# The values of the last two tiles of batch 0: by transfers into block-diagonal chunk slots instead of shift products

## The chip, the cores and the metric

The kernel runs on 1 core of one Trainium2 chip. The metric is device time in microseconds (us), as the median of several runs. A profile is one execution of its own; its time is told beside its span (first to last recorded instruction).

## What is computed

Chunked attention, then a gated feed-forward (B=4 batches, H=8 heads, S=768 rows, D=64; chunks of 32 rows):

```python
for c in range(S // 32):
    c_start = 32 * c
    l_start, r_end = max(0, c_start - 16), min(S, c_start + 32 + 8)
    k_full = concatenate([mem_k, k[:, :, l_start:r_end]], axis=2)   # 8 memory rows
    v_full = concatenate([mem_v, v[:, :, l_start:r_end]], axis=2)
    scores = (q_c @ k_full.T) / sqrt(D)
    out[:, :, c_start:c_start + 32] = softmax(scores) @ v_full
x = out.transpose(0, 2, 1, 3).reshape(3072, 512)
y = (relu(x @ w_gate) * (x @ w_val)) @ w_out                        # 512 -> 1536 -> 512
```

## The kernel before

**Tiles and blocks.** Attention is done in 24 tiles of 128 rows (4 chunks each, 6 tiles per batch, all 8 heads at once). The feed-forward takes blocks of 2, 2, 2, 4, 4, 4, 4 and 2 tiles. Blocks 0 and 1 (tiles 0 to 3) run interleaved by groups of hidden chunks (`GROUPS`, line 52), so that each part of the weights is used by both as it arrives; then come their output products, then block 2 (tiles 4 and 5), block 3 (tiles 6 to 9) and so on.

**A tile's steps.** q and k are transposed on TensorE (lines 239, 280), scores go to PSUM (line 311), VectorE and ScalarE do the softmax (lines 324 to 354), p is transposed (line 360), `values` multiplies it with v (lines 376 to 390), and `x_copy` writes the block's input. `first` (line 409) makes the gate and value products, `relu` and `gate` (lines 415, 421) read them, `second` (line 434) makes the output products with `w_out`.

**v.** A chunk needs 56 rows of context plus 8 memory rows for each of two heads: 128 partitions for a pair of heads. For batches 1 to 3 `v_bd[b % 2]` holds, per head pair and chunk, a block-diagonal 128x128 matrix, filled by transfers (`load_v_rows`), copies on chip (`upper`) and the memory rows (`mem_rows`); `values` then needs one product per pair and chunk, 16 per tile (line 390). Batch 0 goes another way: `load_v_tile` (line 201) brings v in natural order, 128 rows at a time; `shift` (line 217) multiplies it with a shifted band matrix so that each chunk's context starts at partition 0 or 64; `shift_copy` writes the result to `v_q`, which lies inside `v_bd[0]`. `values` then does 4 products with the pattern of the memory rows `vmem_0` (line 376) and 32 products with `v_q` (line 383) per tile. `v_bd[0]` must be zero outside the slots before batch 2 uses it: the `z0` operations (line 136 or 134) do that, those of head pairs 2 and 3 early, those of 0 and 1 after `values` of tile 5.

**The order of the work.** Everything is written in an order that a small planner in the kernel (`schedule`, line 700) works out: each operation has engines with planned durations, a priority, dependencies, and rooms of buffers that it takes and gives. Engines execute their streams in that order; TensorE gets `idle_product`s in planned gaps up to 18 us. Loads are a list of their own, issued in order by GpSimd (POOL in the profile): q and k of batch 0 as pairs of tiles (`load_pair`, tag `qk_p`), v tiles, weights by group (`load_gate_val`), memory values, then the steps of `ORDER` (line 55), in which an integer is so many q or k loads of later tiles, `w0` and `w1` are the two halves of `w_out`, `v1` is v of batch 1. The planner takes a load as landed a fixed time after its turn on the queue; for a load that is neither a gate weight nor `vl`, that time is 2.4 up to the 44th load and 4.0 behind it (line 758). The v and q/k loads share 8 buffers (tag `qk_b`).

Of the kernel before, what the change touches and what calls it, by code (L numbers as in the profile page):

```python
# [11 lines left out]
BF16 = mybir.dt.bfloat16  # L12
# [7 lines left out]
def kernel(  # L20
# [12 lines left out]
    nc = tc.nc  # L33

    B, H, S, D = q.shape
# [5 lines left out]
    CH = 32  # L41
    NCH = S // CH
    HP = H // 2
    TPB = S // 128
# [4 lines left out]
    CTX = 16 + CH + 8  # L49
    NSET = 2  # L50
# [1 line left out]
    GROUPS = [(0, 2), (2, 6), (6, 9), (9, 12)]  # L52
    BAND0 = 48
    UT = 3
    ORDER = [5, 'w0', 'w1', 'v1', 15, 'v2', 'm2', 6, 'v3', 10, 'm3']

    LATE_QK, LATE_P = 11, 10

# [3 lines left out]
    const = ctx.enter_context(tc.tile_pool(name="const", bufs=1))  # L62
# [15 lines left out]
    def copy(eng, o, i):  # L78
        if eng is nc.scalar:
            nc.scalar.copy(o, i)  # L80
        else:
            eng.tensor_copy(o, i)  # L82


    band = const.tile([128, BAND0 + 176], F16, name="band")
    ident_h = band[:, BAND0:BAND0 + 128]
    ident_b = const.tile([128, 128], BF16, name="ident_b")
    idle = const.tile([128, 256], BF16, name="idle")
    ident_f = const.tile([128, 128], F32, name="ident_f")
    w_gate_sb = const.tile([128, NFC, DFF], F16, name="w_gate_sb")  # L90
    w_val_sb = const.tile([128, NFC, DFF], F16, name="w_val_sb")
# [4 lines left out]
    vmem_0 = const.tile([128, HP, 2 * D], F16, name="vmem_0")  # L96
    v_bd = [const.tile([128, HP, NCH, 2 * D], F16, name=f"v_bd_{s}") for s in range(NSET)]
    vmem_f = v_bd[0][:, HP - 1].rearrange("p c d -> p (c d)").bitcast(F32)[:, 0:HP * 2 * D].rearrange(
        "p (h d) -> p h d", h=HP)
    v_q = v_bd[0][:, 0:2].rearrange("p h c d -> p (h c d)").rearrange("p (h c d) -> p h c d", h=HP, d=D)  # L100
    v_n = {}
    warm = const.tile([1, 8], F32, name="warm")

# [34 lines left out]
    def idle_product(N):  # L138
        if "idle" not in TMP:
            TMP["idle"] = fps.tile([128, 512], F32, tag="fps", name="idle_ps")  # L140
        nc.tensor.matmul(TMP["idle"][:, 0:N], lhsT=idle[:, 0:128], rhs=idle[:, 0:N], start=True, stop=True)  # L141
# [55 lines left out]
    def load_v_tile(t):  # L197
        if t % 2 == 0:
            x = ldpool.tile([128, 2, H, D], F16, tag="qk_b", name="v_n")
            v_n[t], v_n[t + 1] = x[:, 0], x[:, 1]  # L200
        nc.gpsimd.dma_start(
            v_n[t],
            bass.AP(tensor=v.tensor, offset=v[0, 0, 128 * t, 0].offset,
                    ap=[[D, 128], [S * D, H], [1, D]]))

    def shift(c0):
        ps = TMP["sh", c0] = fps.tile([128, 2, HP, D], F32, tag="fps", name="vs_ps")
        for i in range(2):
            t, g = divmod(c0 + i, 4)
            parts = [(t, BAND0 + CH * g - 16)]  # L210
            if g == 0 and t:
                parts.append((t - 1, BAND0 + 112))
            if g == 3 and t < TPB - 1:
                parts.append((t + 1, BAND0 - 48))
            for n, (src, x) in enumerate(parts):
                for par in range(2):
                    nc.tensor.matmul(ps[D * par:D * par + D, i], lhsT=band[:, x:x + 64],  # L217
                                     rhs=v_n[src][:, HP * par:HP * par + HP, :],
                                     start=(n == 0), stop=(n == len(parts) - 1))

    def shift_copy(c0, eng):
# [148 lines left out]
    def values(a):  # L370
        b, t = divmod(a, TPB)
        ps = TMP["x", a] = aps.tile([128, HP, 128], F32, tag="aps", name="xT_ps")
        x = PT.pop(a)
        if b == 0:
            for hp in range(HP):
                nc.tensor.matmul(ps[:, hp, :], lhsT=vmem_0[:, hp, :], rhs=x[:, hp, :],  # L376
                                 start=(hp == 0), stop=False, skip_group_check=True)
            for hp in range(HP):
                for g in range(4):
                    r = slice(CH * g, CH * g + CH)  # L380
                    for par in range(2):
                        p = D * par
                        nc.tensor.matmul(ps[p:p + D, hp, r], lhsT=v_q[p:p + CTX, hp, 4 * t + g, :],  # L383
                                         rhs=x[p:p + CTX, hp, r], start=False, stop=(hp, g) == (HP - 1, 3),
                                         skip_group_check=True)
            return
        for hp in range(HP):
            for g in range(4):
                r = slice(CH * g, CH * g + CH)
                nc.tensor.matmul(ps[:, hp, r], lhsT=v_bd[b % NSET][:, hp, 4 * t + g, :],  # L390
                                 rhs=x[:, hp, r], start=True, stop=True)

    def x_copy(a, eng):
# [59 lines left out]
    def op(key, eng, fn, deps=(), prio=(0,), take=(), give=(), after=()):  # L453
        ops[key] = dict(eng=eng, fn=fn, deps=list(deps), prio=prio, take=list(take), give=list(give),
                        after=list(after))

    def load(key, n, work, fn, deps=(), take=(), after=()):
        loads.append(dict(key=key, n=n, work=work, fn=fn, deps=list(deps), take=list(take), after=list(after)))
# [7 lines left out]
    engine = {"ACT": nc.scalar, "DVE": nc.vector}  # L466
# [3 lines left out]
    op("idle", {"DVE": 0.2}, lambda e: nc.vector.memset(idle, 0.0), prio=(-10,))  # L470
    for hp in range(HP):
        op(("z1", hp), {"ACT": 1.5} if hp % 2 else {"DVE": 1.4}, lambda e, hp=hp: zero(engine[e], v_bd[1], hp), ["idle"], prio=(-1, hp), after=["warm2", "vmem_f"] + ["ib"] * (hp == 2))
    for hp in (2, 3, 0, 1):
        for c0 in range(0, NCH, 8):
            op(("z0", hp, c0), {"ACT": 0.6, "DVE": 0.55}, lambda e, hp=hp, c0=c0: zero(engine[e], v_bd[0], hp, c0, c0 + 8),
               ["vm0" if hp > 1 else ("v", TPB - 1)], prio=(3, -hp) if hp > 1 else (0.7, hp),
               after=[("v", 3)] + ([("tc", 12, 1)] if (hp, c0) == (1, NCH - 8) else []))
    op("warm", {"DVE": 0.15}, lambda e: nc.vector.memset(warm, 0.0), prio=(-9,))  # L478
    op("warm2", {"ACT": 1.5}, lambda e: nc.scalar.activation(warm, warm, ACT.Exp), ["warm"], prio=(-9,))
    op("vmem_f", {"DVE": 0.55}, lambda e: nc.vector.memset(vmem_f, 0.0), prio=(-8,), after=["warm"])  # L480
# [45 lines left out]
    for a in range(NT):  # L526
# [38 lines left out]
            op(("pc", a), psum16(HP * 128), lambda e, a=a: p_copy(a, engine[e]), [("p", a)], (1, a, 9), ["pT"], ["aps"])  # L565
        else:
            op(("pc", a), {"SP": ISSUE}, lambda e, a=a: p_transfer(a), [("nrm", a)], (0, a), ["pT"], [("pn", min(LAND_P[a], 7.0))])
        if b == 0:
            for c0 in (4 * t, 4 * t + 2):
                need = {c // 4 for c in (c0, c0 + 1)} | {max(c0 - 1, 0) // 4, min(c0 + 2, NCH - 1) // 4}  # L570
                gone = ([t - 1] if c0 % 4 == 0 and t in (2, 4) else []) + ([t] if c0 == NCH - 2 else [])
                op(("sh", c0), {"PE": 0.4}, lambda e, c0=c0: shift(c0), [("vn", n) for n in sorted(need)] + ["ident"],
                   (1, a, 7.5), ["fps"], ["qk"] * len(gone), [("s", t)])
                op(("shc", c0), {"ACT": psum(2 * HP * D)["ACT"]} if t < 2 else psum(2 * HP * D), lambda e, c0=c0: shift_copy(c0, engine[e]), [("sh", c0)],
                   (1, a, 7.6), (), ["fps"], [("exp", 0)] if t == 0 else [])
        blk = block_of[a]
        j = a - starts[blk]
        op(("v", a), {"PE": 0.45 if b else 1.0}, lambda e, a=a: values(a),
           [("pc", a) if a < LATE_P else (("pc", a), LAND_P[a])]
           + ([("vl", b, n) for n in range(2)] + [("up", b, n, m) for n in range(2 * HP) for m in range(t // UT + 1)]  # L580
              + [("ve", b, n) for n in range(2) if last] if b else [("shc", 4 * t), ("shc", 4 * t + 2), "vm0"])
           + ([("mr", b, n) for n in range(2 * HP)] if b else []), (1, a, 10), ["aps"] + (["xT"] if j == 0 else []), ["pT"],
           [("v", a - 1)] if a else [])
        op(("x", a), psum(HP * 128), lambda e, a=a: x_copy(a, engine[e]), [("v", a)], (1, a, 11), (), ["aps"],
# [3 lines left out]
    for rank, (blk, m) in enumerate(seq):  # L588
        n = BLOCKS[blk]
# [44 lines left out]
    def load_w_op(g):  # L634
        for w in range(2):
            for par in range(2):
                load(("w", g, w, par), 256, 0.35 * (GROUPS[g][1] - GROUPS[g][0]), lambda g=g, w=w, par=par: load_gate_val(g, w, par))

    def load_pair_op(r, i):
        load(("pl", r, i), 1024, 1.45, lambda: load_pair(r, i), take=["qk"])  # L640

    def load_v_nat(t):
        load(("vn", t), 1024, 1.05, lambda: load_v_tile(t), take=["qk"] * (1 - t % 2))

    late = [(a, i) for a in range(TPB, NT) for i in (1, 0)]
    load_pair_op(0, 1)
# [10 lines left out]
    load_v_nat(4)  # L657
    load_w_op(1)
    load_w_op(2)
    load_w_op(3)  # L660
    load_pair_op(2, 0)
    load_v_nat(5)
    for par in range(2):
        load(("vm", par), 256, 0.3, lambda par=par: mem_values(par))
    def v_deps(b):
# [34 lines left out]
    def schedule():  # L700
# [31 lines left out]
        while len(started) < len(ops) + len(loads):  # L732
# [8 lines left out]
            while moved:  # L741
                moved = False
                for e in ("POOL", "PE", "ACT", "DVE", "SP"):
# [18 lines left out]
                    else:  # L762
# [7 lines left out]
                            soon = soon or ready(ops[key], t + (0.45 if t < WARM + 4.0 else 0.3))  # L770
                        if o is None:
                            if e == "PE" and 1.3 < t < WARM:
                                order.append((t, lambda: idle_product(256)))
                                free[e] = t + (0.213 if t < 9.0 else 0.11)
                                heapq.heappush(times, free[e])
                            elif e == "PE" and t <= 1.3:
                                heapq.heappush(times, 1.31)
                            continue
# [65 lines left out]
```

## Time and profile before

| | us |
|---|---|
| median of 3 runs (range) | 240.51 (239.97 to 242.75) |
| the profiled execution: its own time | 240.21 |
| its span | 238.4 |
| TensorE (PE) busy | 231.5 |
| VectorE (DVE) busy | 146.3 |
| ScalarE (ACT) busy | 134.7 |
| GpSimd (POOL) busy, nearly all of it issuing transfers | 77.4 |

A row of the timeline has start, duration, engine, line, operation, output<-inputs, the number of instructions merged into it, and in brackets the idle time before it with what ended it. A row of the chain of waits has start, length, and what the time went to. "PEld" is TensorE's load of stationary operands, which runs beside the products. "DMA to landing" counts from the issue of a transfer to its arrival.

### The profile page before, as it was taken

How to read it: one execution, taken by the hardware profiler on the slowest of the kernel's cores; microseconds unless marked ns; L12 is line 12 of the kernel's file. 1: busy time of each engine (PE TensorE's matmuls, PEld its weight loads, DVE VectorE, ACT ScalarE, POOL GpSimd, SP SyncE). 2: the span in 40 equal slices, each digit the busy share in tenths (PEclk: the TensorE clock that was granted, in tenths of full speed). 3: DMA queues.
4: the chain of work that ended last, by engine and by line, in shares of the span. 5: the costliest groups of instructions: out<-in, count | busy, mean ns of one | idle time of the engine just before them, and what ended most of it. 6: DMA issues, size and time to landing. Idle time of an engine off the chain costs nothing.

```text
span 238.4 us, 6425 instructions
## 1 busy us (share of the span) xinstructions
PE 231.5 (97%) x2649; PEld 135.9 (57%) x2649; DVE 146.3 (61%) x293; ACT 134.7 (57%) x283; POOL 77.4 (32%) x102
## 2 busy tenths in 40 slices
PE   6898999999999999999999999999999999999994
PEld 4576887885579644454544444444545444445873
DVE  6578677997798389993179860399982043410430
ACT  6595766876875385995464953476621233312422
POOL 8975679414910074460086643000000000000000
PEclk9999999999999999999999999999999999999999
DMA  6999999999999969999389999922121200012102
GB/s 68 171 180 200 201 170 162 191 142 117 199 161 157 126 102 145 81 132 193 118 88 134 139 144 120 220 78 47 29 44 64 114 1 0 0 45 90 44 3 88
DMA packets 103069, 26.88 MB, mean 113 GB/s; under 512 B 94080, under 2 KB 99968, under 8 KB 103040
## 3 DMA queue, kind: packets, MB, share of 16 engines
q0 software_dynamic: 76128, 14.65, 90.1%
q1 hardware_dynamic: 23312, 5.53, 20.5%
q10 hardware_dynamic: 3600, 6.29, 8.1%
q8 instruction: 21, 0.34, 0.7%
q14 instruction: 8, 0.07, 0.1%
HBM read 28.55 MB, written 6.29 MB: 146 GB/s over the span
## 4 chain that ended last, share of the span: by engine, by line
PE 93%; DMA 2%; DVE 1%; POOL 1%; issue 1%; ACT 1%; ACTq 0%; POOLq 0%
PE v_ps L409 27%; PE g_ps L409 26%; PE out_ps L434 26%; PE xT_ps L390 3%; PE s_ps L311 2%; DMA qk_p<-in_k_dram 2%; PE vs_ps L217 2%; PE idle_ps L141 2%; PE xT_ps L383 1%; PE qk_ps L280 1%; PE pT_ps L360 1%; PE qk_ps L239 1%; POOL qk_p L230 1%; PE xT_ps L376 1%; ACT o_sb L80 0%
## 5 line engine op out<-in xcount | busy, mean ns | idle before, releaser
L409 PE MATMUL g_ps<-xT,w_gate_sb 128*128 128x256 f16 (+1 forms) x384 | 78.3, 326 | 0.9 <-DVE xT L82 0.4
L409 PE MATMUL v_ps<-xT,w_val_sb 128*128 128x256 f16 (+1 forms) x384 | 78.2, 326 | 0.0
L421 DVE TENSOR_TENSOR gvT<-v_ps,g_relu 128x256 f16<-128x256 f32 (+1 forms) x96 | 52.8, 552 | 40.6 <-PE v_ps L409 28.1
L415 ACT ACTIVATE g_relu<-g_ps 128x256 f16<-128x256 f32 (+1 forms) x96 | 46.9, 491 | 41.4 <-PE g_ps L409 39.9
L434 PE MATMUL out_ps<-w_out_sb,gvT 128*128 128x512 f16 (+2 forms) x300 | 65.8, 371 | 0.0
L409 PEld LDWEIGHTS <-w_gate_sb 128*128 128x128 f16 x384 | 36.9, 98 | 26.1 <-issue 1.4
L409 PEld LDWEIGHTS <-w_val_sb 128*128 128x128 f16 x384 | 35.8, 98 | 22.2 <-issue 0.2
L434 PEld LDWEIGHTS <-gvT 128*128 128x128 f16 x300 | 27.7, 98 | 29.6
L80 ACT COPY o_sb<-out_ps 128x512 f32<-128x512 f32 (+2 forms) x25 | 14.1, 566 | 34.6 <-PE out_ps L434 26.6
L324 DVE TENSOR_REDUCE mx<-s_ps 128x8 f32<-128x512 f32 x24 | 16.5, 686 | 15.3 <-PE s_ps L311 15.1
L339 ACT ACTIVATE p_exp<-dif 128x256 f16<-128x256 f32 (+2 forms) x72 | 19.6, 339 | 5.8 <-DVE dif L331 4.9
L185 POOL DMA_DIRECT2D v_bd<-in_v_dram x12 | 11.0, 934 | 33.2 <-ACT v_bd L134 18.1
L258 POOL DMA_DIRECT2D qk_b<-in_k_dram x18 | 16.2, 902 | 9.4 <-DMA v_bd<-in_v_dram 4.1
L80 ACT COPY v_bd<-v_bd 24x768 f16<-24x768 f16 (+1 forms) x23 | 18.3, 820 | 1.6 <-ACT o_sb L80 1.3
L258 POOL DMA_DIRECT2D qk_b<-in_q_dram x18 | 16.3, 906 | 8.2 <-DMA v_bd<-in_v_dram 6.2
L343 DVE TENSOR_REDUCE sm<-p_exp 128x8 f32<-128x512 f16 x24 | 16.3, 678 | 2.4 <-ACT p_exp L339 2.3
L354 DVE TENSOR_TENSOR p_n<-p_exp,rinv 128x512 f16<-128x512 f16 x24 | 16.4, 685 | 0.3
L331 DVE TENSOR_TENSOR dif<-s_ps,mx 128x512 f32<-128x512 f32 x24 | 16.2, 673 | 0.3
L168 POOL DMA_DIRECT2D v_bd<-vmem x16 | 10.1, 642 | 12.5 <-DMA v_bd<-in_v_dram 6.3
L390 PEld LDWEIGHTS <-v_bd 128*128 128x128 f16 x288 | 9.8, 96 | 3.6
L80 ACT CAST xT<-xT_ps 128x512 f16<-128x512 f32 x13 | 7.6, 585 | 6.2 <-PE xT_ps L390 5.4
L141 PE MATMUL idle_ps<-idle 128*128 128x256 bf16 x64 | 10.1, 304 | 1.1 <-DVE warm L478 1.1
(61 smaller groups left out, 167.1 us busy)
## 6 DMA issues: line engine op xcount, KB each, us to landing
out_dram<-o_sb ACTq DMA_DIRECT2D x23, 256.0 KB
qk_b<-in_k_dram POOLq DMA_DIRECT2D x18, 128.0 KB, 7.6
qk_b<-in_q_dram POOLq DMA_DIRECT2D x18, 128.0 KB, 8.6
v_bd<-in_v_dram POOLq DMA_DIRECT2D x6, 384.0 KB, 11.3
w_out_sb<-in_moe_w_out_dram POOLq DMA_DIRECT2D x2, 768.0 KB, 10.5
qk_p<-in_k_dram POOLq DMA_DIRECT2D x3, 256.0 KB, 5.5
qk_p<-in_q_dram POOLq DMA_DIRECT2D x3, 256.0 KB, 5.9
v_n<-in_v_dram POOLq DMA_DIRECT2D x6, 128.0 KB, 6.8
```

What stands on the lines that cost most here:

```text
L80: nc.scalar.copy(o, i)
L258: nc.gpsimd.dma_start(qk_b[a][:, 1 - i], bass.AP(tensor=x.tensor, offset=x[b, 0, 128 * t, 0].offset, ap=[[D, 128], [S * D, H], [1, D]]))
L324: nc.vector.reduce_max(SM[a, "mx"], s4, axis=AX.X)
L331: nc.vector.tensor_tensor(out=SM[a, "dif"].rearrange("p (m r) a s -> p r m a s", r=2), in0=S_ps.pop(a).rearrange("p r (m a) s -> p r m a s ...
L339: nc.scalar.activation(p[:, :, :, s0:s0 + k1 - k0], dif[:, :, :, k0:k1], ACT.Exp, scale=SCALE)
L343: nc.vector.reduce_sum(SM[a, "sm"], SM[a, "p"], axis=AX.X)
L354: nc.vector.tensor_tensor(out=P_n[a], in0=SM.pop((a, "p")), in1=rinv_b, op=ALU.mult)
L390: nc.tensor.matmul(ps[:, hp, r], lhsT=v_bd[b % NSET][:, hp, 4 * t + g, :], rhs=x[:, hp, r], start=True, stop=True)
L409: nc.tensor.matmul(ps, lhsT=w[:, f, 128 * m:128 * m + 128], rhs=xTs[blk][:, f, :], start=(f == 0), stop=(f == NFC - 1))
L415: nc.scalar.activation(st["r", m], st.pop((0, m)), ACT.Relu)
L421: nc.vector.tensor_tensor(out=st["gv"][:, m, :], in0=st.pop((1, m)), in1=st.pop(("r", m)), op=ALU.mult)
L434: nc.tensor.matmul(st["o", t, c], lhsT=st["gv"][:, m, 128 * t:128 * t + 128], rhs=w_out_sb[:, m, c[0]:c[1]], start=(m == 0), stop=(m == ND ...
```

## The change

Tiles 0 to 3 of batch 0 (`EDGE = 4`) keep their way. For tiles 4 and 5 (chunks 16 to 23, `NQ = 16`) there is a new part `v_e` of `v_bd[0]` with 8 block-diagonal 128x128 slots per head pair. `spread` (one per pair, on VectorE) copies `vmem_0[:, hp]`, which is zero but for the memory rows, into all 8 slots; `load_v_ctx` (two per pair, 8 in all) brings the 56 context rows of the 8 chunks into place by transfer. `values` of tiles 4 and 5 takes the 16 products of line 390, and their shifts and shift copies are gone. v tile 4 is loaded with 16 rows only (tile 3's last shift needs them), v tile 5 not at all. The pair load of q for tiles 4 and 5 moves ahead of the last weight group; the new loads come behind that group. One q/k load moves from behind `w_out` to ahead of it. The zeroing of head pair 2 moves behind `values` of tile 5, since `v_e` reaches into that pair's slots. Up to 9 us of planned time idle products are 512 wide instead of 256, and the zeroed `idle` tile is 512 wide. The diff, cut to its core:

```diff
-    ORDER = [5, 'w0', 'w1', 'v1', 15, 'v2', 'm2', 6, 'v3', 10, 'm3']
+    EDGE = 4
+    ORDER = [6, 'w0', 'w1', 'v1', 14, 'v2', 'm2', 6, 'v3', 10, 'm3']
-    idle = const.tile([128, 256], BF16, name="idle")
+    idle = const.tile([128, 512], BF16, name="idle")
+    NQ = 4 * EDGE
+    v_e = v_flat[:, HP * NQ * D:HP * NQ * D + HP * (NCH - NQ) * 2 * D].rearrange("p (h c d) -> p h c d", h=HP, d=2 * D)
...
+    def spread(hp, eng):
+        x = vmem_0[:, hp]
+        copy(eng, v_e[:, hp], bass.AP(tensor=x.tensor, offset=x.offset, ap=[x.ap[0], [0, NCH - NQ], [1, 2 * D]]))
+
+    def load_v_ctx(hp, par):
+        nc.gpsimd.dma_start(
+            v_e[64 * par:64 * par + CTX, hp, :, D * par:D * par + D],
+            bass.AP(tensor=v.tensor, offset=v[0, HP * par + hp, CH * NQ - 16, 0].offset,
+                    ap=[[D, CTX], [CH * D, NCH - NQ], [1, D]]))
...
-        if b == 0:
+        if b == 0 and t < EDGE:
             for hp in range(HP):
                 nc.tensor.matmul(ps[:, hp, :], lhsT=vmem_0[:, hp, :], rhs=x[:, hp, :],
...
-                nc.tensor.matmul(ps[:, hp, r], lhsT=v_bd[b % NSET][:, hp, 4 * t + g, :],
+                nc.tensor.matmul(ps[:, hp, r], lhsT=v_bd[b % NSET][:, hp, 4 * t + g, :] if b else v_e[:, hp, 4 * t + g - NQ, :],
...
-    for hp in (2, 3, 0, 1):
+    for hp in (3, 2, 0, 1):
...
-               ["vm0" if hp > 1 else ("v", TPB - 1)], prio=(3, -hp) if hp > 1 else (0.7, hp),
+               ["vm0" if hp > 2 else ("v", TPB - 1)], prio=(3, -hp) if hp > 2 else (0.7, hp),
+    for hp in range(HP):
+        op(("ze", hp), {"DVE": 0.66}, lambda e, hp=hp: spread(hp, engine[e]), ["vm0"], prio=(3, hp), after=[("tc", 1, 0)])
...
-        if b == 0:
+        if b == 0 and t < EDGE:
             for c0 in (4 * t, 4 * t + 2):
...
     load_w_op(2)
+    load_pair_op(2, 0)
     load_w_op(3)
-    load_pair_op(2, 0)
-    load_v_nat(5)
+    for hp in range(HP):
+        for par in range(2):
+            n = CTX * (NCH - NQ)
+            load(("vd", hp, par), n, n * 1.03e-3, lambda hp=hp, par=par: load_v_ctx(hp, par), (), (), [("ze", hp)])
...
-                                order.append((t, lambda: idle_product(256)))
+                                n = 512 if t < 9.0 else 256
+                                order.append((t, lambda n=n: idle_product(n)))
```

More of the change, by code (lines that the diff above doesn't have):

```diff
@@ L99 @@
         "p (h d) -> p h d", h=HP)
-    v_q = v_bd[0][:, 0:2].rearrange("p h c d -> p (h c d)").rearrange("p (h c d) -> p h c d", h=HP, d=D)
+    v_flat = v_bd[0].rearrange("p h c d -> p (h c d)")
+    NQ = 4 * EDGE
+    v_q = v_flat[:, 0:HP * NQ * D].rearrange("p (h c d) -> p h c d", h=HP, d=D)
+    v_e = v_flat[:, HP * NQ * D:HP * NQ * D + HP * (NCH - NQ) * 2 * D].rearrange("p (h c d) -> p h c d", h=HP, d=2 * D)
     v_n = {}
@@ L200, in load_v_tile @@
             v_n[t], v_n[t + 1] = x[:, 0], x[:, 1]
+        n = 128 if t < EDGE else 16
         nc.gpsimd.dma_start(
-            v_n[t],
+            v_n[t][0:n],
             bass.AP(tensor=v.tensor, offset=v[0, 0, 128 * t, 0].offset,
-                    ap=[[D, 128], [S * D, H], [1, D]]))
+                    ap=[[D, n], [S * D, H], [1, D]]))
+    def spread(hp, eng):
[6 more added lines that the diff above has]
+                    ap=[[D, CTX], [CH * D, NCH - NQ], [1, D]]))
     def shift(c0):
@@ L216, in shift @@
                 for par in range(2):
-                    nc.tensor.matmul(ps[D * par:D * par + D, i], lhsT=band[:, x:x + 64],
-                                     rhs=v_n[src][:, HP * par:HP * par + HP, :],
+                    k = slice(0, 128 if src < EDGE else 16)
+                    nc.tensor.matmul(ps[D * par:D * par + D, i], lhsT=band[k, x:x + 64],
+                                     rhs=v_n[src][k, HP * par:HP * par + HP, :],
                                      start=(n == 0), stop=(n == len(parts) - 1))
@@ L567 @@
             op(("pc", a), {"SP": ISSUE}, lambda e, a=a: p_transfer(a), [("nrm", a)], (0, a), ["pT"], [("pn", min(LAND_P[a], 7.0))])
-        if b == 0:
+        if b == 0 and t < EDGE:
             for c0 in (4 * t, 4 * t + 2):
                 need = {c // 4 for c in (c0, c0 + 1)} | {max(c0 - 1, 0) // 4, min(c0 + 2, NCH - 1) // 4}
-                gone = ([t - 1] if c0 % 4 == 0 and t in (2, 4) else []) + ([t] if c0 == NCH - 2 else [])
+                gone = [t] * ((c0 == 8) + 2 * (c0 == NQ - 2))
                 op(("sh", c0), {"PE": 0.4}, lambda e, c0=c0: shift(c0), [("vn", n) for n in sorted(need)] + ["ident"],
@@ L577 @@
         j = a - starts[blk]
-        op(("v", a), {"PE": 0.45 if b else 1.0}, lambda e, a=a: values(a),
+        op(("v", a), {"PE": 0.45 if a >= EDGE else 1.0}, lambda e, a=a: values(a),
            [("pc", a) if a < LATE_P else (("pc", a), LAND_P[a])]
            + ([("vl", b, n) for n in range(2)] + [("up", b, n, m) for n in range(2 * HP) for m in range(t // UT + 1)]
-              + [("ve", b, n) for n in range(2) if last] if b else [("shc", 4 * t), ("shc", 4 * t + 2), "vm0"])
+              + [("ve", b, n) for n in range(2) if last] if b else [("vd", hp, par) for hp in range(HP) for par in range(2)] if t >= EDGE else [("shc", 4 * t), ("shc", 4 * t + 2), "vm0"])
            + ([("mr", b, n) for n in range(2 * HP)] if b else []), (1, a, 10), ["aps"] + (["xT"] if j == 0 else []), ["pT"],
@@ L642, in load_v_nat @@
     def load_v_nat(t):
-        load(("vn", t), 1024, 1.05, lambda: load_v_tile(t), take=["qk"] * (1 - t % 2))
+        n = 1024 if t < EDGE else 8 * 16
+        load(("vn", t), n, n * 1.03e-3, lambda: load_v_tile(t), take=["qk"] * (1 - t % 2))
     late = [(a, i) for a in range(TPB, NT) for i in (1, 0)]
@@ L772, in schedule @@
                             if e == "PE" and 1.3 < t < WARM:
-                                order.append((t, lambda: idle_product(256)))
-                                free[e] = t + (0.213 if t < 9.0 else 0.11)
+                                n = 512 if t < 9.0 else 256
+                                order.append((t, lambda n=n: idle_product(n)))
+                                free[e] = t + (0.213 if t < 9.0 else 0.11) * n / 256
                                 heapq.heappush(times, free[e])
```

## The prediction

> **What bounds the kernel now.** I read the page's busy times and slices first, then the chain that ended last, then that chain piece by piece around tiles 4 and 5, then POOL's timeline.
>
> ```profile
> PE 231.5 (97%) x2649; PEld 135.9 (57%) x2649; DVE 146.3 (61%) x293; ACT 134.7 (57%) x283; POOL 77.4 (32%) x102
> ...
> PE   6898999999999999999999999999999999999994
> ...
> PEclk9999999999999999999999999999999999999999
> ...
> PE 93%; DMA 2%; DVE 1%; POOL 1%; issue 1%; ACT 1%; ACTq 0%; POOLq 0%
> ```
>
> TensorE is busy in every slice but the first and last, at full granted clock, and holds 93% of the chain. So work taken from TensorE behind the start is worth its length, if what it then reaches sooner is there. The pieces in question, in the chain of waits:
>
> ```profile
> 39.38 0.78 PE vs_ps L217 x12
> ...
> 41.59 0.67 PE vs_ps L217 x10
> ...
> 52.52 0.22 PE xT_ps L376 x4
> 52.74 0.61 PE xT_ps L383 x32
> 53.35 0.75 PE out_ps L434 x3
> ```
>
> Shifts (L217) and values (L376 with L383) of tiles 4 and 5 stand on the path as TensorE work. At 53.35 the first output product starts: the next thing that needs a transfer not used before, `w_out`. What 16 block-diagonal products cost is seen a little later in the same view:
>
> ```profile
> 62.69 0.39 PE xT_ps L390 x16
> ```
>
> POOL's timeline:
>
> ```profile
> 25.40 0.61 POOL L111 DMA_DIRECT2D w_val_sb<-in_moe_w_val_dram  x1 [0.67 <-DMA w_val_sb<-in_moe_w_val_dram]
> 26.65 0.89 POOL L230 DMA_DIRECT2D qk_p<-in_q_dram  x1 [0.64 <-PE s_ps L311]
> 27.93 0.89 POOL L201 DMA_DIRECT2D v_n<-in_v_dram  x1 [0.39 <-issue]
> 28.81 1.35 POOL L158 DMA_DIRECT2D vmem<-in_mem_v_dram  x2
> 30.58 0.91 POOL L258 DMA_DIRECT2D qk_b<-in_k_dram  x1 [0.42 <-PE v_ps L409]
> ...
> 36.34 1.65 POOL L125 DMA_DIRECT2D w_out_sb<-in_moe_w_out_dram  x2
> ...
> 45.44 0.88 POOL L258 DMA_DIRECT2D qk_b<-in_q_dram  x1 [2.01 <-DMA w_out_sb<-in_moe_w_out_dram]
> 49.81 0.87 POOL L258 DMA_DIRECT2D qk_b<-in_k_dram  x1 [3.49 <-DMA w_out_sb<-in_moe_w_out_dram]
> ```
>
> POOL issues in order, and behind 18 us each issue starts when the eighth transfer before it has landed: the issue at 45.44 follows the first half of `w_out`, the one at 49.81 the second. The landings of `w_out`:
>
> ```profile
> DMA to landing us min/median/max: 8.8/10.5/12.1
> ```
>
> The halves land at 36.34 + 8.8 = 45.1 and 37.17 + 12.1 = 49.3. The output products want them from 53.35, the second half six products (6 x 0.215 = 1.3) later: over 5 us of room.
>
> **The change part by part.**
>
> Shifts: 22 products go, 0.78 + 0.67 = 1.45 us of TensorE, all on the path. Their copies on ACT (two rows of two, 1.07 and 1.09) lay beside full TensorE: nothing.
>
> Values: per tile 0.22 + 0.61 = 0.83 becomes 0.39, twice: 0.88. By distances between starts in the timeline it is 0.93 against 0.40, so the two parts could be worth 2.5 instead of 2.33. I take 2.33.
>
> Spreads: four VectorE copies of 1024 16-bit elements, not in the trace. Nearest is the copy of memory keys (768 elements, 0.30 to 0.46, median 0.36): times 4/3, 0.40 to 0.61 each, 1.6 to 2.4 in all. They may run from 9.1 us, behind q of tile 1, at the lowest priority. VectorE is busy 8.2 of the 11.9 us from 9.1 to 21.0, so 3.7 are free, in gaps of 1.19, 0.83, 0.55 and 0.88. Cost between nothing and 2.4 (all of it delaying the softmax of tiles 0 and 1, which leads to the first gate product at 21.70). As the gaps are longer than a copy, I take 0.2. A gain is not excluded: TensorE stands still 0.44 (for DVE's xT) and 0.41 ("issue") between 21 and 22.6, and another order might lose these: -0.85 at most.
>
> Idle products and tile: the wider memset costs (0.485 - 0.17)/384 x 128 = 0.10 on VectorE at 0.84 us, the doubled products up to 0.21 more wait at an arrival (an idle product takes 0.228 at first, about 0.12 later). Before every q/k transpose up to 9.44 TensorE waits for its transfer by 0.17 to 0.53: it costs nothing, 0.2 with that cover gone.
>
> Zeroing of pair 2: three operations of 0.49 to 0.62 move from 33.75 to behind tile 5, where from 53.3 to 66.7 DVE has 3.1 and ACT 3.3 us free. v of batch 2 waits for a zeroing at 83.86 anyway. Nothing; with that cover gone, 1.7 on the fill of batch 1.
>
> Queue and POOL: v tile 4 shrinks and v tile 5 goes; each took 0.9 of landing time (pair load of q 34.95, v tile 5 35.83). So gate weights behind land 0.9 earlier; the last group, now behind the pair load (1.95 from the landing before), ends at about 33.7 instead of 33.0, for use near 47. Eight context loads have 448 rows of 256 bytes each. POOL's cost is between 0.63 (256 pieces) and 0.89 (1024): 0.69, 5.5 in all; on the queue 448/1024 x 0.9 = 0.39, 3.1 in all, so POOL is the slower. With the rule of eight, the first is issued at 26.2, when the second transfer of weight group 2 lands, the next at 27.5, 28.2, 29.9, 30.8, 31.8, 32.7, and the last ends at 34.4; they land by 39 and are needed at about 47. Memory values follow to 35.75, then six q/k loads at 0.89: `w_out` is issued at 41.1 and 41.9 instead of 36.34 and 37.17, 4.8 later. SP's eight memory-row transfers (36.41, waiting for the memory values) slip some 5 us and stay ahead of tile 6's values (62.69). v of batch 1 slips 4.8; its second half landed at 58.6, and block 3 (85.6) needs tile 9, whose values stand at 79.15. That cover is 5.8 - 2.1 = 3.7 us, against 4.8 if tile 9 hung on it alone: nothing, else 1.1.
>
> `w_out`: the load ahead of it (q/k, issued 40.2) lands five us later as its like did (35.47 to 40.5), so 45.2; the halves took 4.6 and 4.2 from there: 49.8 and 54.0. TensorE is at the output products at 53.35 - 2.33 + 0.2 = 51.2 and at the second half at 52.5. The first is in time, the second 1.5 late. It is no gap if other products stand there. Block 2's first two hidden chunks (4 x 0.44 = 1.76) need only tiles 4 and 5, whose q now lands some 5 us sooner; and the planner counts `w_out` as its 45th and 46th load instead of 37th and 38th, so it allows 4.0 instead of 2.4 for landing and will put ready work first. Bounds 0 and 1.5; I take 0.
>
> Sum against the profiled execution: 240.21 - 1.45 - 0.88 + 0.2 = 238.1. That execution stands 0.30 below the median of the runs, so I say 238.2 for the median. One per cent of the median, about what a measurement can tell from no change, is 2.4 us: the line is 238.1.
>
> **Rivals.**
>
> *B, `w_out` late.* The order holds no filler at the second half: 1.5 us of gap, 238.1 + 1.5 = 239.6. For it: the 4.8 us of POOL. Against: the filler above. If the queue paces the loads instead of POOL, `w_out` slips only by 3.1 - 1.8 + 0.9 = 2.2 and the second half lands at 51.5, in time.
> The Trainium skill, "DMA: Bandwidth & Descriptors", section Bandwidth, calls transfers under 64 KB dominated by descriptors and measures 0.95 us for 64 KB; eight of these (57 KB written) would by that take 7.6 us, 2.1 more than POOL's 5.5, and B would be 241.7. The row of this case (0.9 for twice that size) speaks against it.
>
> *C, slower.* The spreads have the lowest priority on VectorE; if the order puts them late, POOL stands before the first context load with every later load behind it. The lowest-priority memsets now run at 33.75. There the first spread ends at 34.2, the eight loads end at 39.8 instead of 34.4, and the second half of `w_out` lands 5.4 later, at 59.4, 6.9 behind its use; less 1.76 of filler, 238.1 + 5.1 = 243.2. Against it: the gaps from 9.1 on. It turns to a loss against before once the first context load is issued some 2.7 us late (238.1 + 1.5 + 2.7 - 1.76 = 240.5), that is behind 28.9.
>
> *D, the spreads on the start.* All four, at 0.61, delay the softmax of tiles 0 and 1: 238.1 - 0.2 + 2.4 = 240.3. Against it: the four gaps.
>
> **How the numbers follow.** Forecast 0.58, B 0.20, C 0.12, D 0.10. The forecast's own range is 236.9 (2.5 saved, 0.85 gained at the start) to 239.2 (1.1 for block 3). Somewhat over half of it lies below 238.1: faster 0.32. The rest of it, 0.26, with B and D makes "same" 0.56; C makes slower 0.12. The range for 8 in 10 goes from 236.9 to 241.0: all but C and a little on either side.
>
> **What would show it.** Right: 46 products on L217 instead of 68; 16 on L390 for tiles 4 and 5 in about 0.4; first gate product within 0.3 of 21.70; first output product near 51.2; no gap of PE over 0.3 behind 24 us. B: PE idle in front of an output product that waits for `w_out`. C: POOL idle before the first context load, with a VectorE copy as releaser. D: first gate product behind 22.5. I am wrong if PE shows new idle time elsewhere, or the time is outside 236.9 to 241.0.

## The result and the profile after

The changed kernel takes 238.91 us (238.63 to 239.62, 14 runs) against 240.5 (239.86 to 242.75, 14 runs): a ratio of 0.9928, 95% interval 0.9909 to 0.9947: 1.6 us less by the medians, 1.7 by the ratio. Its profiled execution took 239.02 us, with a span of 237.2. In two experiments many runs had TensorE's granted clock halved for a few us (all six of narrow_more_instructions, 0.986 to 0.993 in the mean, and five of the twelve of contexts_behind_w_out_6, 0.991 to 0.993), so their times hold that loss too, and of their profiled executions only the waits and their places are read.

The page after: busy times, TensorE by slices, and the chain by engine.

```profile
PE 230.6 (97%) x2576; PEld 133.4 (56%) x2576; DVE 144.1 (61%) x289; ACT 137.3 (58%) x287; POOL 82.2 (35%) x109
...
PE   7998999989999999999999999999999999999994
...
PE 77%; DMA 11%; POOL 6%; ACT 2%; issue 2%; DVE 1%; ACTq 0%; POOLq 0%
```

TensorE is as full as before, with 73 products fewer. New is the middle of the chain: it runs through POOL's issues into a transfer of `w_out`. TensorE's timeline after, tiles 4 and 5 and the first output products:

```profile
47.05 0.56 PE L406 MATMUL xT_ps<-pT,v_bd 128*128 128x32 f16 x16
...
47.89 0.56 PE L406 MATMUL xT_ps<-pT,v_bd 128*128 128x32 f16 x16
...
50.04 0.60 PE L425 MATMUL v_ps<-xT,w_val_sb 128*128 128x256 f16 x4
51.34 0.82 PE L450 MATMUL out_ps<-w_out_sb,gvT 128*128 128x512 f16 x3 [0.70 <-DMA w_out_sb<-in_moe_w_out_dram]
...
52.45 1.46 PE L450 MATMUL out_ps<-w_out_sb,gvT 128*128 128x512 f16 x6
...
53.97 0.81 PE L450 MATMUL out_ps<-w_out_sb,gvT 128*128 128x512 f16 x3
...
54.95 0.61 PE L425 MATMUL g_ps<-xT,w_gate_sb 128*128 128x256 f16 x4
55.77 0.81 PE L450 MATMUL out_ps<-w_out_sb,gvT 128*128 128x512 f16 x3 [0.21 <-DMA w_out_sb<-in_moe_w_out_dram]
```

The values of tiles 4 and 5 are 16 products each (line 406; 0.41 to the next start). The first output product starts at 51.34 instead of 53.28, but only after a wait: the value products of 50.04 are 0.43 long by starts, so TensorE was ready at 50.47. The second half of `w_out` is waited for again. Ahead of it stand 12 output products with the first half, transposes and scores of later tiles, and one group of gate products at 54.95. POOL's timeline and the landings of `w_out` after:

```profile
27.08 1.48 POOL L216 DMA_DIRECT2D v_bd<-in_v_dram  x2 [0.67 <-DVE dif L347]
...
34.35 0.71 POOL L216 DMA_DIRECT2D v_bd<-in_v_dram  x1 [0.20 <-issue]
...
36.37 0.94 POOL L274 DMA_DIRECT2D qk_b<-in_k_dram  x1
...
41.62 1.72 POOL L129 DMA_DIRECT2D w_out_sb<-in_moe_w_out_dram  x2
```

```profile
DMA to landing us min/median/max: 9.7/11.5/13.3
```

The halves are issued at 41.62 and 42.43 and land at 51.3 and 55.7; before it was 45.1 and 49.3.

Where the 1.2 us between the two profiles come from, by starts of the same product in both:

| | before | after | difference |
|---|---|---|---|
| first gate product | 21.70 | 21.98 | +0.28 |
| third group of gate and value products | 23.15 | 23.08 | -0.07 |
| first output product | 53.28 | 51.34 | -1.94 |
| last output product | 235.10 | 233.91 | -1.19 |

Up to the third group nothing is gained or lost. From there to the first output product 1.87 are gained, net of the wait for `w_out`. Behind it 0.75 are lost again: 0.38 between starts at the second half of `w_out`; for the other 0.37 the trace offers short waits of TensorE at 66 to 68 us, but the order of the products differs there, so this is not shown.

### The profile page after: what moved, and what is told of

The parts are those of the page before. It is cut to its first block, busy times and chain, and to the rows that moved or that the text cites. A ratio compares the mean times of both kernels' runs of the same rounds, so it can differ in the third digit from the quotient of the medians.

```text
span 237.2 us, 6306 instructions
## 1 busy us (share of the span) xinstructions
PE 230.6 (97%) x2576; PEld 133.4 (56%) x2576; DVE 144.1 (61%) x289; ACT 137.3 (58%) x287; POOL 82.2 (35%) x109
## 4 chain that ended last, share of the span: by engine, by line
PE 77%; DMA 11%; POOL 6%; ACT 2%; issue 2%; DVE 1%; ACTq 0%; POOLq 0%
PE out_ps L450 25%; PE v_ps L425 23%; PE g_ps L425 23%; DMA w_out_sb<-in_moe_w_out_dram 6%; DMA w_gate_sb<-in_moe_w_gate_dram 3%; PE xT_ps L406 3%; DMA w_val_sb<-in_moe_w_val_dram 2%; POOL qk_b L274 2%; PE s_ps L327 2%; POOL qk_p L246 1%; POOL v_n L206 1%; POOL v_bd L216 1%; PE pT_ps L376 1%; ACT o_sb L81 1%; PE qk_ps L296 0%
## 5 line engine op out<-in xcount | busy, mean ns | idle before, releaser
L425 PEld LDWEIGHTS <-w_val_sb 128*128 128x128 f16 x384 | 36.4, 98 | 23.5 <-issue 0.2
L425 PEld LDWEIGHTS <-w_gate_sb 128*128 128x128 f16 x384 | 36.0, 98 | 23.6 <-issue 0.3
L81 ACT CAST xT<-xT_ps 128x512 f16<-128x512 f32 x18 | 10.5, 584 | 9.7 <-PE xT_ps L406 7.9
L406 PEld LDWEIGHTS <-v_bd 128*128 128x128 f16 x320 | 10.7, 96 | 3.9 <-issue 0.3
L145 PE MATMUL idle_ps<-idle 128*128 128x256 bf16 (+1 forms) x53 | 11.2, 355 | 1.2 <-DVE warm L496 1.2
```

The source lines that it names most:

```text
L425: nc.tensor.matmul(ps, lhsT=w[:, f, 128 * m:128 * m + 128], rhs=xTs[blk][:, f, :], start=(f == 0), stop=(f == NFC - 1))
```

## The experiments

Each is an edit to the changed kernel, but for before_with_wide_idle. A time is the median of the run, and a ratio is to the kernel before, measured beside it. Most edits also change the order that the planner writes, from the first us on, so a run seldom tests one load or one wait alone.

**no_context_loads.** What is the gain without the transfers? The list of loads loses its eight, and the values of tiles 4 and 5 wait for the spreads instead of them:

```diff
-            load(("vd", hp, par), n, n * 1.03e-3, lambda hp=hp, par=par: load_v_ctx(hp, par), (), (), [("ze", hp)])
```

> The changed kernel without its eight context loads; it leaves out the context rows in the values of tiles 4 and 5 (their slots hold the memory rows alone), with the same products. Theory 1 (TensorE saves about 2.3 us, and about 1.2 of it are lost because the w_out halves, held back by POOL's eight issues, land behind the first output products): POOL issues w_out some 5.5 us sooner, both waits at the output products go, 237.7 us. Theory 2 (the missing part is lost elsewhere, at the start or behind 60 us): 238.9 as with the loads.

238.28 us, 0.9892 (0.9853 to 0.9930). TensorE and POOL in its timeline:

```profile
50.52 0.81 PE L450 MATMUL out_ps<-w_out_sb,gvT 128*128 128x512 f16 x3
```

```profile
34.84 1.69 POOL L129 DMA_DIRECT2D w_out_sb<-in_moe_w_out_dram  x2
```

Both waits for `w_out` are gone. But 0.63 us come back, not 1.2: of the room, part turns into other waits, of 0.36, 0.21 and 0.35 between starts at 65 to 68 us. So the change without its transfers is worth 0.0108 x 240.7 = 2.6 us (1.7 to 3.5 by the interval), and the transfers cost 0.6 to 0.9 of that: 0.6 by the medians, where the runs do not overlap (238.02 to 238.55 against 238.63 to 239.62), and 0.9 by the two ratios, whose intervals do.

**five_ahead_of_w_out, four_ahead_of_w_out, w_out_first.** If POOL's issues ahead of `w_out` are the loss, fewer of them should bring it back.

```diff
-    ORDER = [6, 'w0', 'w1', 'v1', 14, 'v2', 'm2', 6, 'v3', 10, 'm3']
+    ORDER = [5, 'w0', 'w1', 'v1', 15, 'v2', 'm2', 6, 'v3', 10, 'm3']
```

and `[4, 'w0', 'w1', 'v1', 16, ...]`, `['w0', 'w1', 6, 'v1', 14, ...]`.

> One edit to the changed kernel: five q/k loads ahead of w_out as in the kernel before, not six. Theory 1: w_out is issued 0.9 us sooner and lands near 50.4 and 54.8 instead of 51.3 and 55.7; the wait of 0.70 at the first output product goes nearly, the second of 0.21 too: 238.0 us. Theory 2: 238.9.

239.98 us, 0.9980 (0.9951 to 1.0009).

> Four q/k loads ahead of w_out. Theory 1: w_out 1.8 us sooner, near 49.5 and 53.9; no wait at output products, 237.8 us, unless the q/k load of tile 8 that is moved behind w_out is now what an engine waits for. Theory 2: 238.9.

241.91 us, 1.0035 (1.0010 to 1.0061).

> No q/k load ahead of w_out. Theory 1: w_out 5.4 us sooner, near 46 and 50, no wait at output products: 237.7 us, less what the q/k loads of tiles 6 and 7, now about 8 us later, cost in new waits (between 0 and 1 us). Theory 2: 238.9.

242.99 us, 1.0108 (1.0070 to 1.0146).

All three expectations failed by 2 to 5 us, in a row: the sooner `w_out`, the slower. TensorE with five loads ahead:

```profile
65.92 0.38 PE L296 MATMUL qk_ps<-ident_b,qk_b 128*128 128x128 bf16 x4 [0.74 <-ACT qT L81]
...
82.84 0.55 PE L406 MATMUL xT_ps<-pT,v_bd 128*128 128x32 f16 x16
84.18 1.02 PE L425 MATMUL g_ps<-xT,w_gate_sb 128*128 128x512 f16 x4 [0.78 <-DVE xT L83]
```

The wait at the first output product (50.61 here) is gone as expected. In its place stand 0.74 at a q transpose, and 0.78 at block 3, whose first gate product now follows the values of tile 9 directly; in the changed kernel 12 output products stood between them. With four ahead:

```profile
51.16 0.81 PE L450 MATMUL out_ps<-w_out_sb,gvT 128*128 128x512 f16 x3
54.26 2.53 PE L450 MATMUL out_ps<-w_out_sb,gvT 128*128 128x512 f16 x11 [2.29 <-DMA w_out_sb<-in_moe_w_out_dram]
```

Here the planner puts the output products in long rows, presumably expecting `w_out` sooner (the row at 54.26 is cut off by the window), and the second half lands at 54.2 only. With none ahead TensorE waits twice for q/k transfers among the output products (0.92 and 0.89) and 1.45 at the values just ahead of block 3. My theory, that the loss is a late `w_out` that fewer loads ahead of it would mend, fell: in each of these orders other waits came in its place and cost more.

**contexts_behind_w_out_6 and _7.** The eight loads go behind `w_out` instead; tiles 4 and 5 are needed only by block 2.

```diff
+    ORDER = [6, 'w0', 'w1', 'd0', 'v1', 14, 'v2', 'm2', 6, 'v3', 10, 'm3']
+        elif kind == "d":
+            for hp in range(HP):
+                for par in range(2):
+                    ...
+                    load(("vd", hp, par), n, n * 1.03e-3, lambda hp=hp, par=par: load_v_ctx(hp, par), (), (), [("ze", hp)])
```

> The eight context loads move behind both halves of w_out; six q/k loads ahead of it as in the changed kernel. Tiles 4 and 5 are then finished among the output products of blocks 0 and 1, which is in time for block 2. Theory 1 (what is lost at w_out is the eight issues of POOL ahead of it): w_out issued at about 36, landed by 49; no wait at the output products, 238.2 us as without the context loads. Rival (any order of POOL's work only moves the wait, as with fewer q/k loads ahead): a new wait of 0.5 us or more on a q/k transpose, on a value product of tile 4 or at block 2, 238.9 us or more.

241.03 us, 1.0030 (1.0004 to 1.0056).

> As the last, with seven q/k loads ahead of w_out: w_out issued at about 37, landed by 50, no wait there; one more q/k load lands early, so two transposes of tile 9 or 10 can stand among the output products. Theory 1: 238.2 us. Rival: 238.9 us or more by a new wait elsewhere.

240.21 us, 0.9996 (0.9976 to 1.0016). The rival held in both. No wait for `w_out` (first output product at 49.62 and 49.50, against 51.34 in the changed kernel), but with six ahead, at block 3:

```profile
82.60 0.55 PE L406 MATMUL xT_ps<-pT,v_bd 128*128 128x32 f16 x16
84.76 1.62 PE L425 MATMUL g_ps<-xT,w_gate_sb 128*128 128x512 f16 x4 [1.61 <-ACT xT L81]
```

Four gate products that take 1.02 in the run with five loads ahead take 1.62 here, with the granted clock at 0.50 to 0.53 from 85 to 88 us. With seven ahead TensorE waits 0.82 for a relu at 64.9 us, and at block 3 0.52 ahead of tile 9's values and 0.43 behind them. What was gained at 50 us is lost again, much of it where tile 9 feeds block 3. That stage was in my prediction, as a cover of 3.7 us that would hold.

**short_lag.** Was the filler ahead of the second half due to the planner's landing time of 4.0?

```diff
-... else 2.4 if n_load < 45 else ...
+... else 2.4 if n_load < 53 else ...
```

> The planner's landing time of 2.4 us reaches to the 52nd load instead of the 44th, so that w_out is planned 1.6 us sooner in the changed kernel; loads stay in the same order. Theory 1 (the planner's allowance of 4.0 put filler ahead of the second half of w_out): less filler, the wait at the second half grows from 0.21 to 1 us or more, 239.5 us. Rival (the filler stood there anyway, and the planner is too optimistic either way): waits at the output products of 0.7 and 0.2 as before, 238.9 us.

239.03 us, 0.9932 (0.9911 to 0.9952): the rival. The group of filler stays, and the wait for `w_out` is 0.5 in all. The landing time was not what put it there.

**late_spreads.**

```diff
-prio=(3, hp), after=[("tc", 1, 0)])
+prio=(3, hp), after=[("x", 1)])
```

> The four spreads become eligible only behind the copy of tile 1's attention output, so two of them leave the stretch from 9 to 13 us. Theory A (the spreads lay in idle time of VectorE): first gate product unchanged at 21.98, context loads issued at most 1 us later, 238.9 us within 0.3. Theory B (they delay the softmax of tiles 0 and 1): first gate product 0.3 or more sooner.

239.74 us, 0.9958 (0.9943 to 0.9973). The first gate product stays (21.92), so theory B is out: the spreads do not touch the start. Theory A's time missed too, 0.8 above its 238.9 where it allowed 0.3: the order of the attention steps behind changes, and TensorE waits 0.71 for an x copy of VectorE at 67.4.

**v3_ahead.** In the changed kernel TensorE stood 0.46 for v tile 3 at 19.4, some 2 us ahead of the first gate product (21.98).

```diff
-    load_pair_op(2, 1)
     load_v_nat(3)
+    load_pair_op(2, 1)
```

> One edit to the changed kernel: v tile 3 is loaded ahead of the k pair of tiles 4 and 5 instead of behind it. In the changed kernel TensorE stood 0.46 us at 19.4 for v tile 3, two products into the last shift ahead of tile 1's values. Theory A (the start is set by that transfer): it lands about 1.4 us sooner, the wait goes, the first gate product comes about 0.4 us sooner than 21.98, 238.5 us. Theory B (the start is set by the softmax and the wait only takes the place of another): the first gate product stays within 0.1 of 21.98, 238.9 us.

239.01 us, 0.9935 (0.9910 to 0.9959). The wait goes, the first gate product comes 0.32 sooner (21.66), and the time does not move. Of the 0.32, 0.15 are left at the third group of products (22.93 against 23.08), with a wait of 0.24 put down to "issue" in between. The rest goes at the next stage: `w_out` is waited for until 51.40, against 51.34.

**narrow_idle and before_with_wide_idle.** The widening of the idle products, taken back in the changed kernel, and done alone in the kernel before.

```diff
-    idle = const.tile([128, 512], BF16, name="idle")
+    idle = const.tile([128, 256], BF16, name="idle")
-                                n = 512 if t < 9.0 else 256
+                                n = 256
```

> Idle products 256 wide throughout and the idle tile 256 wide, as before; the rest of the change stays. Theory A (widening costs nothing and gains nothing): first gate product between 21.7 and 22.0, 238.9 us. Theory B (the wide products are what brought the start up to 18.95 forward by 0.37 us): first shift of tile 2's last pair back at 19.3, first gate product near 22.2, 239.2 us.

241.27 us, 1.0032 (1.0006 to 1.0058): 2.4 more than with the widening, all of the gain. Both theories were wrong.

> The kernel before with the idle products of the first 9 us 512 wide, and nothing else of the change. Theory P (the products that the change takes away carry its gain): within 0.4 us of 240.5. Theory W (the widening alone carries the gain, since taking it back in the changed kernel cost 2.4 us): 239.0 or less.

240.72 us, 1.0010 (0.9988 to 1.0033): theory P. So the widening is worth nothing alone, and in this order of the work it decides whether the saved products are worth anything. TensorE in the narrow kernel:

```profile
29.10 0.27 PE L425 MATMUL v_ps<-xT,w_val_sb 128*128 128x256 f16 x1
30.80 0.49 PE L425 MATMUL v_ps<-xT,w_val_sb 128*128 128x256 f16 x3 [1.43 <-issue]
```

```profile
55.26 0.38 PE L296 MATMUL qk_ps<-ident_b,qk_b 128*128 128x128 bf16 x4 [0.73 <-ACT qT L81]
```

Its third group starts at 23.09, as in the changed kernel. Then it loses 1.43 in the middle of four value products, waiting for nothing but issue, and behind the first output product 0.73 and 0.60 at q/k transposes.

**narrow_more_instructions.** Is that gap a matter of how many instructions stand ahead?

```diff
-                                order.append((t, lambda n=n: idle_product(n)))
+                                order.append((t, (lambda: (idle_product(128), idle_product(128))) if t < 4.0 else lambda n=n: idle_product(n)))
```

> The changed kernel with narrow idle products, the first 13 of them as two products of half the width: 13 products and their weight loads more, in the same time, and the same order of everything else. In the narrow kernel TensorE stood 1.43 us inside a group of four value products at 29.4, waiting for nothing but its own issue. Theory F (TensorE's instructions arrive by transfers of 16 KB on queue 8, and the stretch of program that it runs when one is asked for decides whether it waits): the gap moves by 26 instructions, to about 27.7, or shrinks where the small products of tile 2's values stand there; time changes by the gap, 239.9 to 241.3 us. Rival (a data wait at that value product): the gap of 1.4 us stays at the same product, 241.3 us.

244.91 us, 1.0137 (1.0099 to 1.0176). TensorE, around its three gaps:

```profile
21.72 0.20 PE L399 MATMUL xT_ps<-pT,v_bd 56*64 56x32 f16 x2 [1.05 <-issue]
...
30.91 0.23 PE L399 MATMUL xT_ps<-pT,v_bd 56*64 56x32 f16 x4 [0.92 <-issue]
...
78.86 0.28 PE L425 MATMUL g_ps<-xT,w_gate_sb 128*128 128x256 f16 x1 [2.60 <-issue]
```

The gap left the value product and stands in tile 2's values now, and two others came: the rival is out, since no data of those products changed. That it shrinks was half right (0.92), that the time would fall was wrong. How much of the 3.6 us over the narrow kernel the gaps cost is not shown: the granted clock is 0.50 from 22 to 25 us, behind the gap of 1.05, and again from 80 to 83, behind that of 2.60, and there a group of four products starts 0.85 after the last instead of 0.44.

In the traces the gaps have one thing in common: a 16 KB packet on the queue of instructions starts shortly before each ends (28.40 to 30.80 in the narrow kernel; 19.39 to 21.72, 28.59 to 30.91 and 76.36 to 78.86 here; 20.16 to 22.60 in the kernel before). It holds for every "issue" wait that the timelines of TensorE list behind the first us: 14 in 12 of the fourteen traces, each ending 2.27 to 2.50 us after such a packet began. But these traces have 282 such packets, and all the others pass without such a wait. I take the packets for TensorE's own program arriving. That a gap comes when one is asked for too late is argued from these times, not shown.

## Why the prediction was right, and where a term was wrong

The forecast of 238.2 was 0.7 too low; 238.91 lies in its range of 236.9 to 241.0 and in the case "within 1%", which had 0.56. The last step of the sum is a slip: 238.1 and the 0.30 make 238.4, 0.5 below what was measured.

By the prediction's own signs it is rival B that came, with TensorE idle in front of output products that wait for `w_out`, though smaller than the 1.5 us of B. The number stayed close in part by luck, as two errors pulled in opposite ways: TensorE was ready for the first output product 2.81 sooner (50.47 instead of 53.28), where the sum has 2.33 - 0.2 = 2.13; then 1.25 were lost at `w_out` and 0.37 behind it, where the sum has nothing.

**Shifts and values: right.** 46 products are left on the shift line, and tiles 4 and 5 take 16 each. Taking product times from the chain, the work between the first gate product and the first output product falls by 2.58, of which 0.28 are eight transposes done ahead of it: 2.30 against my 2.33. Without the loads the whole kernel gains 2.6. But that the products are worth this needs the wide idle products: with narrow ones the change gains nothing.

**Spreads: harmless, as rated.** They took 0.46, 0.42, 0.38 and 0.42, at the low end of my 0.40 to 0.61. Rivals C and D did not happen: the first context load went out at 27.08, ahead of the 28.9 from which C would have decided.

**`w_out`: the term that failed.** "Bounds 0 and 1.5; I take 0." TensorE waited 0.70 and 0.21, 0.87 and 0.38 between starts: 1.25 in all. This is the mechanism of B, and what was mis-sized is the landing. The halves landed 1.5 and 1.7 later than I worked out: the issue was 0.5 later (first context load at 27.08 instead of 26.2), the way from issue to landing 1.0 and 1.2 longer. The longer way is not the context loads' doing: without them it is 9.3 and 13.2, and with no q/k load ahead of `w_out` 7.6 and 11.0. The filler was larger than I counted, though not the four groups of block 2: TensorE asked for the second half 4.05 us behind the first (51.34 to 55.39), where I had 1.3 and at most 1.76 of filler. Had the halves landed at 49.8 and 54.0, these times leave no wait at either. Together with the 0.63 of no_context_loads, B's direction is shown. None of the five other orders tried got the loss back.

On the price of a context load the Trainium skill and my row disagreed: "DMA: Bandwidth & Descriptors", section Bandwidth, has 0.95 us for 64 KB, and I took POOL's 0.69. Without the eight loads the second half of `w_out` lands at 48.9 instead of 55.7, 6.8 sooner or 0.85 a load. That looks nearer to the Trainium skill's figure but does not bear it out: it holds POOL's issuing, 0.71 to 0.76 a load, and POOL's waits between the issues, 0.20 to 1.13. For the transfer itself the row holds: in the trace of no_context_loads the queue begins some 1,200 packets of 128 bytes in each us from 34 to 37, and at that pace the 448 of a context load take 0.37, an estimate.

**The start: right for a wrong reason.** I allowed 0.2 for spreads and up to -0.85 for another order. In twelve of the fourteen kernels profiled here (the two others are those with narrow idle products in the changed kernel) the first gate product starts between 21.36 and 22.00, and the third group between 22.89 and 23.22 all the same. In ten of the twelve TensorE waits between the two, for 0.17 to 0.69, and the profile puts the wait down to "issue". In the kernel before:

```profile
21.70 0.49 PE L409 MATMUL g_ps<-xT,w_gate_sb 128*128 128x256 f16 x3 [0.44 <-DVE xT L82]
22.60 0.28 PE L409 MATMUL g_ps<-xT,w_gate_sb 128*128 128x256 f16 x1 [0.41 <-issue]
```

It is this wait that takes up most of what comes sooner; of the 0.32 of v tile 3 it took half. No kernel came near the bound of -0.85: the third group is at best 0.26 sooner than before. The bound of 2.4 on the other side was not put to the test.

**Idle products: wrong.** "It costs nothing, 0.2 with that cover gone." I rated the edit by its own time; taking it back costs 2.4 us here. Of the 2.7 between the two profiles, 1.5 are there at the first output product (52.85 against 51.34), with the issue gap of 1.43 ahead of it and in spite of the 0.87 that the changed kernel waits there; 1.2 come behind it. The edit takes 11 products and their weight loads out ahead of everything else, and the planner makes another order of the rest: which of the two it works by was not told apart.

**Block 3's cover: held, but by less than I thought.** In the changed kernel tile 9's copy is covered by 12 output products (80.94 to 83.53, 2.6 us where I had 3.7). With five loads ahead, with none, and with the context loads behind `w_out` that cover was gone, at 0.78, 1.45 and 1.61.

Open: why the planner's order ends well with six loads ahead and wide idle products, and ill in nearly every neighbour tried. Of the eleven edits to the changed kernel none beats it beyond the noise but the one that leaves the loads out. It was not tried to bring the eight context loads together into fewer.

## What to carry to other kernels

When work is taken from a full engine, ask what it reaches sooner and price the transfers in front of that: here 2.3 us of products were saved, TensorE then stood 1.25 at the next weight, and leaving the new transfers out gave 0.6 to 0.9 back. A wait for a late transfer is not always a mistake in the order: if what stands ahead of it in the queue is needed too, moving one load up can move the wait to the one that slipped, as in the five other orders here. And an edit is not free because it has no time of its own: check the number of instructions and the written order that it changes, by taking it back alone.

## What the runs showed of the hardware

TensorE can stand still in the middle of a group of products and wait for nothing that the profile shows: 0.41 at 22.2 us in the kernel before, 1.43 at 29.4 with narrow idle products, 2.60 at 76.3 with 13 more products ahead. The profile puts such a wait down to "issue"; all 14 in these traces ended 2.27 to 2.50 us after a 16 KB packet on the instruction queue (q8 in the page, 20 or 21 packets in a run) began, and most packets pass without one. Adding 13 idle products and their weight loads early in the program, in the same time, moved the long gap and made two others.

TensorE's granted clock was halved three times in these traces ahead of its last product, for 3.4 us each: from 21.9 and from 80.0 in narrow_more_instructions, from 85.1 in contexts_behind_w_out_6. Each time TensorE had stood still shortly before, for 1.05, 2.60 and 1.61 us. Waits of 1.43, 1.45 and 2.29 in the traces of narrow_idle, w_out_first and four_ahead_of_w_out were not followed by a lower clock, so what brings it on is not shown.
